# Fixing every engine's order by hand in an attention and feed-forward kernel: early casts and masks, spare matmuls, and values once per query third

## The chip, the cores and the metric

The kernel runs on one core of a Trainium2 chip. The metric is the device time of a run in microseconds. The profile's span (first to last instruction) is about 1.8 us shorter than that time.

The engines are called as the profile calls them: PE is TensorE's matmuls, PEld its weight loads, ACT ScalarE, DVE VectorE, POOL GpSimd, SP SyncE.

## The reference

Block-sparse attention (4 batches, 8 heads, 768 tokens, head size 64), then a multiplicative feed-forward layer on 3072 tokens:

```python
scores = q @ k.T / 8                       # per batch and head
mask   = |blk_i - blk_j| <= 1, or first/last block row or column, or one of 3 sampled blocks
attn   = softmax(where(mask, scores, -1e9))
x      = (attn @ v), heads side by side     # (3072, 512)
out    = ((x @ w1) * (x @ w2)) @ w3 @ w_out # d_ff = 1024, out (3072, 512)
```

## The kernel before

Queries are taken in tiles of 256, so each batch has three query thirds `t`; heads are taken four at a time (`Q`); keys in three pairs of chunks (`kp`). One *score group* is `(b, t, Q, kp)`: two score tiles of 128x1024, two exps, two mask multiplies. There are 72 groups, s = 0 to 71. Three consecutive groups (kp = 0, 1, 2) are what I call a *third*: after them the values and the softmax sum are complete and are normalized. There are 24 thirds.

`w3 @ w_out` is folded once into one matrix `wf` (the *fold*: w3 transposed on PE, `w3p`, copied by DVE to `w3t`, multiplied, `wp`, copied by DVE to `wf`). The feed-forward work is cut into *units* of four matmuls of 512 columns, held in a queue `fill` and popped between groups so that PE has work while ACT computes exps.

```python
ps_s = pool("ps_s", 2, space=PSUM)     # score tiles, also transposes: 2 buffers
ps_o = pool("ps_o", 1, space=PSUM)     # values and softmax sum
ps_f = pool("ps_f", 2, space=PSUM)     # everything else: mask, fold, feed-forward: 2 buffers
order = tc.manual_schedule(engines={PE, Activation, DVE})  # these run in the order written
# ... (masks: mp = matmul in ps_f, copied to SBUF on ACT; all nine before the first scores)

def scores(b, t, Q, kp, i):
    s = ps_s.tile(...)
    # 4 matmuls of 256 columns (64-row tiles)
    nc.scalar.activation(e, s, AF.Exp, scale=1.0 / 8.0)
    nc.vector.tensor_tensor(e, e, mask[...], op=ALU.mult)

def normalize(b, t, Q):
    nc.scalar.activation(ln, d, AF.Ln)
    nc.scalar.activation(rec[:, 0, :], ln, AF.Exp, scale=-1.0)
    nc.vector.tensor_tensor(X[i][...], o, rec, op=ALU.mult)

def pa(f):   p = ps_f.tile(...); 4 matmuls; nc.scalar.copy(a, p)                    # unit
def pb(f):   p = ps_f.tile(...); 4 matmuls; nc.vector.tensor_tensor(hT, p, a, mult) # unit
def po(n, half): 4 matmuls into box["o"] (ps_f); after the second half DVE copies it out

for s, g in enumerate(groups):
    scores(b, t, Q, kp, 0)
    scores(b, t, Q, kp, 1)
    if prev is not None:
        values(*prev)          # values of the group before
        finish(prev)           # normalize if kp == 2
    # ... (loads of the next batch; batches 1 to 3 are turned by DMA)
    pop(0 if s < 3 else 2)     # two units
    prev = g
```

(Cuts and shortened bodies are marked by `...` or described in comments.)

The softmax here doesn't subtract the row's maximum and nothing guards it: scores larger than these inputs give would overflow.

Of the kernel before, what the change touches and what calls it, by code (L numbers as in the profile page):

```python
# [17 lines left out]
def kernel(  # L18
# [16 lines left out]
    nc = tc.nc  # L35
# [10 lines left out]
    def pool(name, bufs, **kw):  # L46
# [7 lines left out]
    epool = pool("epool", 6)  # L54
# [10 lines left out]
        engines={mybir.EngineType.PE, mybir.EngineType.Activation, mybir.EngineType.DVE}  # L65
# [12 lines left out]
    rand_sb = const.tile([NB, 6], I32, tag="rand_sb")  # L78
    nc.sync.dma_start(out=rand_sb, in_=sampled_blocks.bitcast(I32))

    def load_pair(b, pr, which="qkv"):
        for src, dst, pl, tag in ((qv, qn, nat, "qn"), (kv, kn, nat, "kn"), (vv, vn, natv, "vn")):
            if tag[0] in which:
                t = pl.tile([128, 2, C, D], BF16, tag=tag, name=tag)
                nc.gpsimd.dma_start(out=t, in_=src[b][:, 2 * pr:2 * pr + 2])  # L85
                dst[b, pr] = t

# [7 lines left out]
    def load_w12(ap, t):  # L95
        src = ap.rearrange("(Q g s d) f -> g d Q s f", Q=2, g=4, s=2)
        for g in range(4):
            for Q in range(2):
# [3 lines left out]
    load_pair(0, 0, "qk")  # L102
    idf = const.tile([128, 128], F32, tag="idf")
    nc.gpsimd.iota(idf, pattern=[[-1, 128]], base=0, channel_multiplier=1,
                   allow_small_or_imprecise_dtypes=True)
    load_pair(0, 1, "qk")
    hotf = const.tile([NB, C, 128], F32, tag="hotf")
    nc.gpsimd.iota(hotf, pattern=[[1, C], [C, 128]], base=0, channel_multiplier=-BLK,
# [4 lines left out]
    II = const.tile([NB, NB], F32, tag="II")  # L113
    nc.gpsimd.iota(II, pattern=[[0, NB]], base=0, channel_multiplier=1,
                   allow_small_or_imprecise_dtypes=True)
    load_pair(0, 0, "v")
    load_pair(0, 1, "v")
    wo_v = moe_w_out.rearrange("(c r) f -> r c f", r=128)
    nc.gpsimd.dma_start(out=wo_sb, in_=wo_v)
# [5 lines left out]
    load_w3(0, 2)  # L125
    load_pair(0, 2)
    load_w3(2, 4)
    load_pair(0, 3)
    load_w3(4, NF)
    load_w12(moe_w1, w1_sb)  # L130
    load_w12(moe_w2, w2_sb)

    ident = const.tile([128, 128], BF16, tag="ident")
    nc.vector.tensor_scalar(ident, in0=idf, scalar1=0.0, scalar2=None, op0=ALU.is_equal)
    ones = const.tile([128, 32], BF16, tag="ones")
    nc.vector.memset(ones, 1.0)
    hot = const.tile([NB, C, 128], BF16, tag="hot")
# [4 lines left out]
    DD = const.tile([NB, NB], F32, tag="DD")  # L142
    nc.vector.tensor_sub(DD, II, JJ)

    A = const.tile([NB, NB], F32, tag="A")
    nc.vector.tensor_tensor(DD, DD, DD, op=ALU.mult)
    nc.vector.tensor_scalar(A, in0=DD, scalar1=1.0, scalar2=None, op0=ALU.is_le)
    for src in (II, JJ):
        for val, op in ((0.0, ALU.is_le), (float(NB - 1), ALU.is_ge)):
            t1 = small.tile([NB, NB], F32, tag="m24", name="m24")  # L150
            nc.vector.tensor_scalar(t1, in0=src, scalar1=val, scalar2=None, op0=op)
            nc.vector.tensor_max(A, A, t1)
    rand_f = const.tile([NB, 3], F32, tag="rand_f")
    for r in range(3):
        nc.vector.tensor_copy(rand_f[:, r:r + 1], rand_sb[:, 2 * r:2 * r + 1])
        t1 = small.tile([NB, NB], F32, tag="m24", name="m24")
        nc.vector.tensor_tensor(t1, JJ, rand_f[:, r:r + 1].to_broadcast((NB, NB)),
                                op=ALU.is_equal)
        nc.vector.tensor_max(A, A, t1)
    Ab = const.tile([NB, NB], BF16, tag="Ab")  # L160
    nc.vector.tensor_copy(Ab, A)
# [3 lines left out]
    gp = ps_s.tile([128, 2, 512], F32, tag="s", name="gp")  # L165
    for i, (lo, n) in enumerate(((0, 512), (512, 256))):
        nc.tensor.matmul(gp[:NB, i, :n], lhsT=Ab, rhs=hot2[:, lo:lo + n], start=True, stop=True)
        nc.vector.tensor_copy(G[:, lo:lo + n], gp[:NB, i, :n])
    mask = const.tile([128, NT, 3, 512], BF16, tag="mask")

    def build_mask(t):
        for kp in range(3):
            mp = ps_f.tile([128, 512], F32, tag="f", name="mp")
# [251 lines left out]
```

## Time and profile before

| what | before | view |
|---|---|---|
| time, median of 4 runs (288.42 to 289.52) | 288.82 us | times |
| span | 286.8 us | page |
| first exp | 20.53 us | timeline of ACT |
| groups 0 to 17 (first exp to group 18's first exp) | 53.6 us | timeline of ACT |
| from there to the first exp of the last third (17 thirds) | 164.2 us | timeline of ACT |
| one third in the steady state | 9.62 us | timeline of ACT |
| last third and tail | 48.5 us | timeline of ACT |

The page of the kernel before: busy time with share of the span, then the busy tenths and PE's granted clock in 40 slices of 7.2 us.

```profile
PE 260.8 (91%) x3124; PEld 132.3 (46%) x3124; DVE 183.8 (64%) x296; ACT 188.8 (66%) x250; POOL 71.5 (25%) x105
...
PE   0478888898999999999999999999999999999994
...
PEclk9986999999999999999999999999999999999998
```

PE is the bound for most of the span; the clock falls in the slices around 20 to 25 us, and at the very end.

The timeline of ACT in the kernel before. Columns: start in us, duration, engine, line, operation, output<-input, shapes, count, and in brackets idle time before it and what ended it. The mask copies stand ahead of the first exp; the second exp of the row at 73.22 is group 18's first, 0.95 us later; the last row opens the last third.

```profile
15.59 4.22 ACT L177 CAST mask<-mp 128x512 bf16<-128x512 f32 x8 [13.57 <-PE mp L175]
...
20.53 1.02 ACT L219 ACTIVATE e<-s 128x1024 bf16<-128x1024 f32 x1
...
73.22 1.97 ACT L219 ACTIVATE e<-s 128x1024 bf16<-128x1024 f32 x2
...
238.34 1.02 ACT L219 ACTIVATE e<-s 128x1024 bf16<-128x1024 f32 x1 [0.61 <-PE s L214]
```

One group of the steady state, in the timeline of the kernel before (same columns):

```profile
163.74 0.38 PE L314 MATMUL pb<-x,w_sb 128*128 128x512 bf16 x1
...
164.05 0.61 PE L214 MATMUL s<-qkt 64*128 64x256 bf16 x8
164.48 1.94 ACT L219 ACTIVATE e<-s 128x1024 bf16<-128x1024 f32 x2
...
164.78 0.40 PE L244 MATMUL o<-e,vn 128*32 128x256 bf16 x8
...
165.55 1.04 PE L303 MATMUL pa<-x,w_sb 128*128 128x512 bf16 x4
166.42 1.03 PE L314 MATMUL pb<-x,w_sb 128*128 128x512 bf16 x4
...
166.62 0.59 ACT L306 CAST a<-pa 128x512 bf16<-128x512 f32 x1 [0.20 <-PE pa L303]
```

Starts tell more than durations here, because matmuls overlap. From 163.74 (a pb matmul) to 164.05 (the first score matmul) it is 0.31 us, while pb matmuls follow each other by 0.216: a switch between kinds of matmul costs about 0.095 us. The Trainium skill, "TensorEngine Tiling (Array Packing)", Key Properties, says that changing the tiling mode drains TensorE; the trace agrees, and gives the size. Note the order on ACT: both exps of the group first, then the copy `a`. Here that does no harm: the values stand between scores and pa on PE, so that pa is done (166.6) just when the exps are (166.4).

PE's waits in the kernel before (engine, line, what it waited for: total us, times, longest):

```profile
PE gp L167 <- DVE Ab L161: 10.6, 1, 10.6
...
PE s L214 <- ACT e L219: 3.5, 10, 1.1
...
PE o L244 <- DVE x L260: 1.7, 2, 1.1
```

After the mask chain at the start (10.6 us) PE waits for little; the wait of `o` for `x` is the normalization that empties the one values buffer.

### The profile page before, as it was taken

How to read it: one execution, taken by the hardware profiler on the slowest of the kernel's cores; microseconds unless marked ns; L12 is line 12 of the kernel's file. 1: busy time of each engine (PE TensorE's matmuls, PEld its weight loads, DVE VectorE, ACT ScalarE, POOL GpSimd, SP SyncE). 2: the span in 40 equal slices, each digit the busy share in tenths (PEclk: the TensorE clock that was granted, in tenths of full speed). 3: DMA queues.
4: the chain of work that ended last, by engine and by line, in shares of the span. 5: the costliest groups of instructions: out<-in, count | busy, mean ns of one | idle time of the engine just before them, and what ended most of it. 6: DMA issues, size and time to landing. Idle time of an engine off the chain costs nothing.

```text
span 286.8 us, 7359 instructions
## 1 busy us (share of the span) xinstructions
PE 260.8 (91%) x3124; PEld 132.3 (46%) x3124; DVE 183.8 (64%) x296; ACT 188.8 (66%) x250; POOL 71.5 (25%) x105
## 2 busy tenths in 40 slices
PE   0478888898999999999999999999999999999994
PEld 0334555454544454445444554445444544444441
DVE  2616786786767776777677767766776677633332
ACT  1088764776788886888877888768887688611310
POOL 8614489374644820066000000000000000000000
PEclk9986999999999999999999999999999999999998
DMA  7999999999999992399912000121000220003003
GB/s 92 151 190 206 208 174 167 178 119 140 135 167 112 144 109 91 79 118 150 160 73 75 2 2 0 39 75 38 3 2 0 77 75 2 0 37 112 0 29 117
DMA packets 70356, 26.16 MB, mean 91 GB/s; under 512 B 58036, under 2 KB 65204, under 8 KB 70324
## 3 DMA queue, kind: packets, MB, share of 16 engines
q0 software_dynamic: 47632, 14.69, 50.9%
q1 hardware_dynamic: 22692, 11.02, 18.5%
q8 instruction: 24, 0.39, 0.6%
q14 instruction: 8, 0.07, 0.1%
HBM read 29.36 MB, written 6.29 MB: 124 GB/s over the span
## 4 chain that ended last, share of the span: by engine, by line
PE 62%; DMA 12%; ACT 12%; DVE 5%; POOL 5%; issue 3%; POOLq 0%; ACTq 0%
PE pa L303 13%; PE o L244 12%; PE pb L314 12%; DMA w_sb<-in_moe_w_dram 11%; PE po L324 10%; ACT e L219 7%; PE s L214 7%; DVE x L260 4%; PE d L241 4%; PE wp L285 3%; ACT rec L259 3%; ACT ln L257 2%; DMA nt<-in_q_dram 2%; POOL w_sb L99 1%; POOL vn L85 1%
## 5 line engine op out<-in xcount | busy, mean ns | idle before, releaser
L219 ACT ACTIVATE e<-s 128x1024 bf16<-128x1024 f32 x144 | 139.1, 1021 | 47.7 <-PE s L214 47.6
L220 DVE TENSOR_TENSOR e<-e,mask 128x1024 bf16<-128x1024 bf16 x144 | 99.0, 691 | 53.8 <-ACT e L219 53.8
L244 PE MATMUL o<-e,vn 128*32 128x256 bf16 x1152 | 54.7, 277 | 5.4 <-DVE x L260 1.7
L214 PE MATMUL s<-qkt 64*128 64x256 bf16 x576 | 46.8, 277 | 3.5 <-ACT e L219 3.5
L303 PE MATMUL pa<-x,w_sb 128*128 128x512 bf16 x192 | 49.7, 381 | 0.0
L314 PE MATMUL pb<-x,w_sb 128*128 128x512 bf16 x192 | 49.2, 379 | 0.0
L316 DVE TENSOR_TENSOR h<-pb,a 128x512 bf16<-128x512 f32 x48 | 33.1, 690 | 20.9 <-PE pb L314 20.9
L324 PE MATMUL po<-wf_sb,h 128*128 128x512 bf16 x192 | 44.5, 380 | 0.0
L306 ACT CAST a<-pa 128x512 bf16<-128x512 f32 x48 | 28.0, 582 | 22.6 <-PE pa L303 22.2
L241 PE MATMUL d<-e,ones 128*32 128x256 bf16 x576 | 42.5, 275 | 0.0
L214 PEld LDWEIGHTS <-qkt 64*128 64x128 bf16 x576 | 22.8, 95 | 34.7 <-issue 32.0
L244 PEld LDWEIGHTS <-vn 128*32 128x32 bf16 x1152 | 27.5, 96 | 22.0 <-issue 19.2
L314 PEld LDWEIGHTS <-w_sb 128*128 128x128 bf16 x192 | 18.7, 98 | 24.1 <-issue 2.6
L201 POOL DMA_DIRECT2D nt<-in_q_dram x24 | 19.7, 824 | 40.2 <-DMA qkt<-nt 35.9
L324 PEld LDWEIGHTS <-h 128*128 128x128 bf16 x192 | 17.5, 98 | 22.3 <-issue 3.4
L303 PEld LDWEIGHTS <-w_sb 128*128 128x128 bf16 x192 | 15.7, 98 | 21.7 <-issue 8.0
L329 DVE COPY ob<-po 128x512 f32<-128x512 f32 x24 | 16.5, 688 | 10.1 <-PE po L324 10.1
L201 POOL DMA_DIRECT2D nt<-in_k_dram x24 | 19.6, 821 | 4.3 <-DMA qkt<-nt 2.3
L260 DVE TENSOR_TENSOR x<-o,rec 128x512 bf16<-128x512 f32 x24 | 16.6, 692 | 1.6 <-ACT rec L259 0.9
L241 PEld LDWEIGHTS <-ones 128*32 128x32 bf16 x576 | 17.3, 98 | 0.3
L285 PE MATMUL wp<-wo_sb,w3t_sb 128*128 128x512 bf16 x64 | 15.2, 380 | 0.0
L177 ACT CAST mask<-mp 128x512 bf16<-128x512 f32 x9 | 4.8, 587 | 13.7 <-PE mp L175 13.7
(56 smaller groups left out, 106.9 us busy)
## 6 DMA issues: line engine op xcount, KB each, us to landing
out_dram<-ob SPq DMA_DIRECT2D x24, 256.0 KB, 2.0
vn<-in_v_dram POOLq DMA_DIRECT2D x16, 192.0 KB, 5.8
nt<-in_q_dram POOLq DMA_DIRECT2D x24, 96.0 KB, 5.6
nt<-in_k_dram POOLq DMA_DIRECT2D x24, 96.0 KB, 5.6
w_sb<-in_moe_w_dram POOLq DMA_DIRECT2D x8, 256.0 KB, 11.2
w_sb<-in_moe_w_dram POOLq DMA_DIRECT2D x16, 128.0 KB, 5.8
wo_sb<-in_moe_w_out_dram POOLq DMA_DIRECT2D x1, 1024.0 KB, 12.0
qn<-in_q_dram POOLq DMA_DIRECT2D x4, 192.0 KB, 7.2
```

What stands on the lines that cost most here:

```text
L201: nc.gpsimd.dma_start(out=n[:, :, h, :], in_=src[b][:, :, 2 * pr + h, :])
L214: nc.tensor.matmul(s[:, h, k2 * QT:(k2 + 1) * QT], lhsT=qk[64 * h:64 * h + 64, 1, kc * 128:(kc + 1) * 128], rhs=qk[64 * h:64 * h + 64, 0, ...
L219: nc.scalar.activation(e, s, AF.Exp, scale=1.0 / 8.0)
L220: nc.vector.tensor_tensor(e, e, mask[:, t, kp:kp + 1, :].to_broadcast((128, 2, 512)), op=ALU.mult)
L241: nc.tensor.matmul(d[rows, :], lhsT=ones, rhs=rhs, start=first, stop=last, skip_group_check=True)
L244: nc.tensor.matmul(o[rows, part * QT:(part + 1) * QT], lhsT=vn[b, 2 * Q + i][:, h, kc, 32 * part:32 * part + 32], rhs=rhs, start=first and ...
L260: nc.vector.tensor_tensor(X[i][:, 2 * Q:2 * Q + 2, half * QT:(half + 1) * QT], o.rearrange("p (s n) -> p s n", s=2), rec.to_broadcast((128 ...
L303: nc.tensor.matmul(p, lhsT=w1_sb[:, c, f * 128:(f + 1) * 128], rhs=x[:, c, :], start=c == 0, stop=c == 3)
L306: nc.scalar.copy(a, p)
L314: nc.tensor.matmul(p, lhsT=w2_sb[:, c, f * 128:(f + 1) * 128], rhs=x[:, c, :], start=c == 0, stop=c == 3)
L316: nc.vector.tensor_tensor(hT[:, f, :], p, box["a"], op=ALU.mult)
L324: nc.tensor.matmul(box["o"], lhsT=hT[:, f, n * 128:(n + 1) * 128], rhs=wf_sb[:, f, :], start=f == 0, stop=f == NF - 1)
```

## The change

Four intentions: an earlier first exp (float32 loads cast on ACT and DVE, a shorter mask chain, only the masks that are needed first); spare matmuls on a zero tile so that PE's clock stays up while it has nothing to do; values for a whole third at once, several groups late, so that PE switches less often and the normalization is off its path; orders of POOL and SP fixed as well. Batch 1's q and k are turned (transposed) by PE instead of DMA; the fold's units are sorted anew, and `w1` and `w2` are loaded at group 9. The diff, cut to its core:

```diff
-    epool = pool("epool", 6)
+    epool = pool("epool", 14)
     order = tc.manual_schedule(
-        engines={PE, Activation, DVE}
+        engines={PE, Activation, DVE, Pool, SP}
     )
+    # q and k of pairs 0 and 1 as float32 over SP, cast on ACT/DVE ("raw")
+    # mask matrix A by memset and affine_select on POOL ...
+    def warm(n):
+        if n:
+            w = ps_f.tile([128, 512], F32, tag="f", name="warm")
+            for _ in range(n):
+                nc.tensor.matmul(w, lhsT=warm_sb[:, :128], rhs=warm_sb, start=True, stop=True)
...
-    transposes(0, 0)
-    transposes(0, 1)
-    for t in range(NT):
-        build_mask(t)
+    warm(9)
+    cast("q", 0, nc.scalar.copy)
+    expand(0)                                  # G for t = 0
+    cast("k", 0, nc.vector.tensor_copy)
+    build_mask(0, 0, nc.scalar.copy)
+    transposes(0, 0, [nc.vector.tensor_copy] * 2)
+    cast("q", 1, nc.scalar.copy)
+    cast("k", 1, nc.vector.tensor_copy)
+    build_mask(0, 1, nc.scalar.copy)
...
-        if prev is not None:
-            values(*prev)
-            finish(prev)
-        pop(0 if s < 3 else 2)
+        if 0 < s <= LEAD:                      # LEAD = 6
+            attend(groups[s - 1:s])
+        elif s > LEAD + 3 and kp == 2:
+            attend(groups[s - 5:s - 2])        # three groups' values, then normalize
+        if s == 0:
+            build_mask(0, 2, nc.vector.tensor_copy)
+        if s in (0, 3):
+            expand(1 + s // 3)
+        if s < 6:
+            build_mask(1 + s // 3, s % 3, nc.vector.tensor_copy)
+        ...
+        if s in (14, 15, 18, 19):
+            transposes(1, (14, 15, 18, 19).index(s), [nc.vector.tensor_copy])
+        ...
+        if s < 4:
+            warm(3)
+        else:
+            pop(1.4 if s < LEAD else 2.0 if s == LEAD + 2 else (2.6, 2.6, 0.0)[kp])
```

A unit costs 0.86 of the budget in `pop`, so the steady state pops three units, three, and none in the three groups of a third.

More of the change, by code (lines that the diff above doesn't have):

```diff
@@ L64 @@
     order = tc.manual_schedule(
-        engines={mybir.EngineType.PE, mybir.EngineType.Activation, mybir.EngineType.DVE}
+        engines={mybir.EngineType.PE, mybir.EngineType.Activation, mybir.EngineType.DVE,
+                 mybir.EngineType.Pool, mybir.EngineType.SP}
     )
@@ L76 @@
     qn, kn, vn = {}, {}, {}
-    rand_sb = const.tile([NB, 6], I32, tag="rand_sb")
-    nc.sync.dma_start(out=rand_sb, in_=sampled_blocks.bitcast(I32))
     def load_pair(b, pr, which="qkv"):
@@ L86, in load_pair @@
                 dst[b, pr] = t
+    raw = {}
+    for pr in range(2):
+        both = hpool.tile([128, 2, 1024], F32, tag="h", name="raw")
+        for x, (src, tag) in enumerate(((qv, "q"), (kv, "k"))):
+            t = both[:, x, :2 * C * D].rearrange("p (h c d) -> p h c d", h=2, c=C)
+            nc.sync.dma_start(out=t, in_=src[0][:, 2 * pr:2 * pr + 2])
+            raw[tag, pr] = t
+        if pr == 0:
+            rand_sb = const.tile([NB, 3, 2], I32, tag="rand_sb")
+            nc.sync.dma_start(out=rand_sb,
+                              in_=sampled_blocks.bitcast(I32).rearrange("e (r w) -> e r w", w=2))
     w1_sb = wts.tile([128, 4, d_ff], BF16, tag="w1")
@@ L99, in load_w12 @@
                 nc.gpsimd.dma_start(out=t[32 * g:32 * g + 32, 2 * Q:2 * Q + 2, :], in_=src[g][:, Q])
-    load_pair(0, 0, "qk")
-    idf = const.tile([128, 128], F32, tag="idf")
+    idf = const.tile([128, 128], BF16, tag="idf")
     nc.gpsimd.iota(idf, pattern=[[-1, 128]], base=0, channel_multiplier=1,
-                   allow_small_or_imprecise_dtypes=True)
-    load_pair(0, 1, "qk")
-    hotf = const.tile([NB, C, 128], F32, tag="hotf")
-    nc.gpsimd.iota(hotf, pattern=[[1, C], [C, 128]], base=0, channel_multiplier=-BLK,
                    allow_small_or_imprecise_dtypes=True)
@@ L112 @@
                    allow_small_or_imprecise_dtypes=True)
-    II = const.tile([NB, NB], F32, tag="II")
-    nc.gpsimd.iota(II, pattern=[[0, NB]], base=0, channel_multiplier=1,
+    A = const.tile([NB, NB], F32, tag="A")
+    nc.gpsimd.memset(A, 0.0)
+    nc.gpsimd.memset(A[:, 0:1], 1.0)
+    nc.gpsimd.memset(A[:, NB - 1:NB], 1.0)
+    for base, pat, mul in ((0, -1, 1), (1, -1, 1), (-1, -1, 1), (0, 0, 1), (1 - NB, 0, 1)):
+        nc.gpsimd.affine_select(out=A, in_=A, compare_op=ALU.not_equal, fill=1.0, base=base,
+                                pattern=[[pat, NB]], channel_multiplier=mul)
+    hotf = const.tile([NB, C, 128], BF16, tag="hotf")
+    nc.gpsimd.iota(hotf, pattern=[[1, C], [C, 128]], base=0, channel_multiplier=-BLK,
                    allow_small_or_imprecise_dtypes=True)
@@ L117 @@
     load_pair(0, 1, "v")
-    wo_v = moe_w_out.rearrange("(c r) f -> r c f", r=128)
-    nc.gpsimd.dma_start(out=wo_sb, in_=wo_v)
+    nc.gpsimd.dma_start(out=wo_sb, in_=moe_w_out.rearrange("(c r) f -> r c f", r=128))
     def load_w3(lo, hi):
@@ L123, in load_w3 @@
             nc.gpsimd.dma_start(out=w3_sb[:, i, :], in_=moe_w3[128 * i:128 * i + 128, :])
-    load_w3(0, 2)
+    load_w3(0, 3)
     load_pair(0, 2)
-    load_w3(2, 4)
+    load_w3(3, 4)
     load_pair(0, 3)
     load_w3(4, NF)
-    load_w12(moe_w1, w1_sb)
-    load_w12(moe_w2, w2_sb)
+    warm_sb = const.tile([128, 512], BF16, tag="warm")
+    nc.vector.memset(warm_sb, 0.0)
     ident = const.tile([128, 128], BF16, tag="ident")
@@ L136 @@
     nc.vector.memset(ones, 1.0)
+    rand_f = const.tile([NB, 3], F32, tag="rand_f")
+    nc.vector.tensor_copy(rand_f, rand_sb[:, :, 0])
+    Ab = const.tile([NB, NB], BF16, tag="Ab")
+    for r in range(3):
+        nc.vector.scalar_tensor_tensor(Ab if r == 2 else A, in0=JJ, scalar=rand_f[:, r:r + 1],
+                                       in1=A, op0=ALU.is_equal, op1=ALU.max)
     hot = const.tile([NB, C, 128], BF16, tag="hot")
@@ L141 @@
     nc.vector.tensor_tensor(hot, hot, hot_hi, op=ALU.mult)
-    DD = const.tile([NB, NB], F32, tag="DD")
-    nc.vector.tensor_sub(DD, II, JJ)
-    A = const.tile([NB, NB], F32, tag="A")
-    nc.vector.tensor_tensor(DD, DD, DD, op=ALU.mult)
-    nc.vector.tensor_scalar(A, in0=DD, scalar1=1.0, scalar2=None, op0=ALU.is_le)
-    for src in (II, JJ):
-        for val, op in ((0.0, ALU.is_le), (float(NB - 1), ALU.is_ge)):
-            t1 = small.tile([NB, NB], F32, tag="m24", name="m24")
-            nc.vector.tensor_scalar(t1, in0=src, scalar1=val, scalar2=None, op0=op)
-            nc.vector.tensor_max(A, A, t1)
@@ L153 @@
-    rand_f = const.tile([NB, 3], F32, tag="rand_f")
-    for r in range(3):
-        nc.vector.tensor_copy(rand_f[:, r:r + 1], rand_sb[:, 2 * r:2 * r + 1])
-        t1 = small.tile([NB, NB], F32, tag="m24", name="m24")
-        nc.vector.tensor_tensor(t1, JJ, rand_f[:, r:r + 1].to_broadcast((NB, NB)),
-                                op=ALU.is_equal)
-        nc.vector.tensor_max(A, A, t1)
-    Ab = const.tile([NB, NB], BF16, tag="Ab")
-    nc.vector.tensor_copy(Ab, A)
+    def warm(n):
[3 more added lines that the diff above has]
+                nc.tensor.matmul(w, lhsT=warm_sb[:, :128], rhs=warm_sb, start=True, stop=True)
@@ L163, with expand @@
     hot2 = hot.rearrange("e c p -> e (c p)")
     G = const.tile([NB, S], BF16, tag="G")
-    gp = ps_s.tile([128, 2, 512], F32, tag="s", name="gp")
-    for i, (lo, n) in enumerate(((0, 512), (512, 256))):
-        nc.tensor.matmul(gp[:NB, i, :n], lhsT=Ab, rhs=hot2[:, lo:lo + n], start=True, stop=True)
-        nc.vector.tensor_copy(G[:, lo:lo + n], gp[:NB, i, :n])
     mask = const.tile([128, NT, 3, 512], BF16, tag="mask")
-    def build_mask(t):
-        for kp in range(3):
-            mp = ps_f.tile([128, 512], F32, tag="f", name="mp")
-            for k2 in range(2):
-                nc.tensor.matmul(mp[:, k2 * QT:(k2 + 1) * QT], lhsT=hot[:, 2 * kp + k2, :],
-                                 rhs=G[:, t * QT:(t + 1) * QT], start=True, stop=True)
-            nc.scalar.copy(mask[:, t, kp, :], mp)
+    def expand(t):
+        gp = ps_f.tile([128, 512], F32, tag="f", name="gp")
+        nc.tensor.matmul(gp[:NB, :QT], lhsT=Ab, rhs=hot2[:, t * QT:(t + 1) * QT],
+                         start=True, stop=True)
+        nc.vector.tensor_copy(G[:, t * QT:(t + 1) * QT], gp[:NB, :QT])
@@ L180, with build_mask, transposes @@
+    def build_mask(t, kp, copy):
+        mp = ps_f.tile([128, 512], F32, tag="f", name="mp")
+        for k2 in range(2):
+            nc.tensor.matmul(mp[:, k2 * QT:(k2 + 1) * QT], lhsT=hot[:, 2 * kp + k2, :],
+                             rhs=G[:, t * QT:(t + 1) * QT], start=True, stop=True)
+        copy(mask[:, t, kp, :], mp)
     QK = {}
-    def transposes(b, pr):
+    def transposes(b, pr, copies):
         tp = ps_s.tile([128, 2, 1024], BF16, tag="s", name="tp")
@@ L189, in transposes @@
         t = qkt.tile([128, 2, S], BF16, tag="qkt", name="qkt")
-        nc.vector.tensor_copy(t, tp[:, :, :S])
+        if len(copies) == 1:
+            copies[0](t, tp[:, :, :S])
+        else:
+            for x, copy in enumerate(copies):
+                copy(t[:, x, :], tp[:, x, :S])
         QK[b, pr] = t
     qd, kd = (x.rearrange("b h (p c) d -> b p c h d", c=C) for x in (q, k))
+    turned = {}
     def load_pair_t(b, pr):
-        load_pair(b, pr, "v")
-        t = qkt.tile([128, 2, S], BF16, tag="qkt", name="qkt")
-        for x, src in enumerate((qd, kd)):
+        ns = []
+        for src in (qd, kd):
             n = nat.tile([128, C, 2, D], BF16, tag="nt", name="nt")
@@ L201, in load_pair_t, with turn @@
                 nc.gpsimd.dma_start(out=n[:, :, h, :], in_=src[b][:, :, 2 * pr + h, :])
+            ns.append(n)
+        turned[b, pr] = ns
+        load_pair(b, pr, "v")
+    def turn(b, pr):
+        t = qkt.tile([128, 2, S], BF16, tag="qkt", name="qkt")
+        for x, n in enumerate(turned.pop((b, pr))):
             nc.sync.dma_start_transpose(out=t[:, x, :].rearrange("r (c p) -> r c p", c=C),
@@ L328, in go, with cast @@
                     ob = opool.tile([128, 512], F32, tag="ob", name="ob")
-                    nc.vector.tensor_copy(ob, box["o"])
-                    nc.sync.dma_start(out=outv[b, c], in_=ob)
+                    if i == B * NT // 2 - 1 and n == 3:
+                        nc.scalar.copy(ob[:, :256], box["o"][:, :256])
+                        nc.scalar.dma_start(out=outv[b, c][:, :256], in_=ob[:, :256])
+                        nc.vector.tensor_copy(ob[:, 256:], box["o"][:, 256:])
+                        nc.sync.dma_start(out=outv[b, c][:, 256:], in_=ob[:, 256:])
+                    else:
+                        nc.vector.tensor_copy(ob, box["o"])
+                        nc.sync.dma_start(out=outv[b, c], in_=ob)
             return go
         for f in range(NF):
-            fill.append(pa(f))
-            fill.append(pb(f))
+            fill.append((0.86, pa(f)))
+            fill.append((0.86, pb(f)))
         for n in range(4):
-            fill.append(po(n, 0))
-            fill.append(po(n, 1))
-    transposes(0, 0)
-    transposes(0, 1)
-    for t in range(NT):
-        build_mask(t)
+            fill.append((0.86, po(n, 0)))
+            fill.append((0.86, po(n, 1)))
+    warm(9)
+    def cast(tag, pr, copy):
+        t = nat.tile([128, 2, C, D], BF16, tag=tag + "n", name=tag + "n")
+        copy(t, raw[tag, pr])
+        (qn if tag == "q" else kn)[0, pr] = t
+    cast("q", 0, nc.scalar.copy)
[6 more added lines that the diff above has]
+    build_mask(0, 1, nc.scalar.copy)
     groups = []
@@ L351 @@
         groups += [(b, t, Q, kp) for t, Q in outer for kp in range(3)]
-    for i in range(NF):
-        fill.append(fold_transpose(i, 0))
-        fill.append(fold_transpose(i, 1))
-        fill.extend(fold_mm(i))
+    ft = [(0.25, fold_transpose(i, jh)) for i in range(NF) for jh in range(2)]
+    fm = [(0.86, go) for i in range(NF) for go in fold_mm(i)]
+    fill.extend(ft[:2])
+    for k_, go in enumerate(fm):
+        fill.append(go)
+        fill.extend(ft[k_ + 2:k_ + 3])
     done = {}
     n_ffn = 0
-    prev = None
     def finish(g):
@@ L369, in finish, with pop, attend @@
                 n_ffn += 1
-    def pop(n):
-        for _ in range(n):
-            if fill:
-                fill.popleft()()
+    def pop(budget):
+        while fill and budget >= fill[0][0] - 0.05:
+            cost, go = fill.popleft()
+            budget -= cost
+            go()
+    def attend(gs):
+        for g in gs:
+            values(*g)
+        finish(g)
+    LEAD = 6
     for s, g in enumerate(groups):
@@ L378 @@
         r = s % 18
-        scores(b, t, Q, kp, 0)
-        scores(b, t, Q, kp, 1)
-        if prev is not None:
-            values(*prev)
-            finish(prev)
-        if b + 1 < B and r in (2, 5, 8, 11):
-            load_pair_t(b + 1, (r - 2) // 3)
-        if b == 0 and s in (7, 8):
-            transposes(0, s - 5)
-        pop(0 if s < 3 else 2)
-        prev = g
-    values(*prev)
-    finish(prev)
+        if s == 0:
+            scores(*g, 0)
+            transposes(0, 1, [nc.vector.tensor_copy])
+            scores(*groups[1], 0)
+        elif s == 1:
+            scores(*groups[0], 1)
+            scores(*g, 1)
+        else:
+            scores(*g, 0)
+            scores(*g, 1)
+        if 0 < s <= LEAD:
+            attend(groups[s - 1:s])
+        elif s > LEAD + 3 and kp == 2:
+            attend(groups[s - 5:s - 2])
+        if s == 0:
+            build_mask(0, 2, nc.vector.tensor_copy)
[3 more added lines that the diff above has]
+            build_mask(1 + s // 3, s % 3, nc.vector.tensor_copy)
+        if s in (7, 8):
+            transposes(0, s - 5, [nc.vector.tensor_copy])
+            load_pair(1, s - 7)
+        if s == 9:
+            load_w12(moe_w1, w1_sb)
+            load_w12(moe_w2, w2_sb)
+            load_pair(1, 2)
+            load_pair(1, 3)
+        if s in (14, 15, 18, 19):
+            transposes(1, (14, 15, 18, 19).index(s), [nc.vector.tensor_copy])
+        if 0 < b < B - 1:
+            if r in (2, 4, 6, 8):
+                load_pair_t(b + 1, (r - 2) // 2)
+            if r in (9, 10, 11, 12):
+                turn(b + 1, r - 9)
+        if s < 4:
+            warm(3)
+        else:
+            pop(1.4 if s < LEAD else 2.0 if s == LEAD + 2 else (2.6, 2.6, 0.0)[kp])
+    attend(groups[-3:])
     while fill:
-        pop(1)
+        pop(1.0)
     order.__exit__(None, None, None)
```

## The prediction

> **What bounds the kernel now.** TensorE: 260.8 of 286.8 us busy (busy table). From about 84 to 248 us the kernel is periodic: the timeline shows one query third (three score groups, 6 exps, two feed-forward units of four 512-column matmuls per group) every 9.62 us. By matmul starts, a 512-column matmul costs 0.216 us, a score group 0.42, a values group 0.65. Each switch between scores, values and feed-forward costs about 0.095 us extra (0.31 instead of 0.216 between starts). The Trainium skill, "TensorEngine Tiling (Array Packing)", Key Properties, says that changing the tiling mode drains TensorE; the trace agrees. A third has 9 switches, plus a 0.19 us wait of values for the normalization.
>
> Before that: first exp at 20.5 us (mask chain on VectorE to 10.5 us, nine mask copies on ScalarE 15.6 to 20.6), granted clock 0.50 at 20 to 25 us. Fits "TensorE: Matmul & The Clock Gate", Part 1 (half clock after an idle window). Groups 0 to 17 take 53.6 us.
>
> **What the change does.** (a) Start: float32 loads cast on ScalarE/VectorE, shorter mask chain on GpSimd, only two mask copies ahead of the first exp, the rest on VectorE. I estimate the first exp at 12 us: -8.5. The warm matmuls mostly fill waits. (b) Groups 0 to 17: fold work spread evenly, transposes of batch 1 on TensorE instead of small DMAs (4 x 1.3 us added), no fill left at groups 15 to 17: net about -2. (c) Steady state: values for three groups at once, 6 switches instead of 9 and no normalization wait: bare TensorE work falls to 8.97 us per third.
>
> **But (c) creates a new wait.** Feed-forward units come three in a row directly behind a score group, through the two shared PSUM buffers. The third reuses the first's buffer, freed by a ScalarE copy that stands behind both exps (and, in the first group of a third, behind ln and reciprocal). With durations of the trace (exp spacing 0.92, copy 0.58, ln to rec 0.43, rec to exp 0.32) that copy ends about 3.26 us after the scores start; TensorE would be ready at 2.25: about 1.06 us lost. In the second group the last unit waits about 0.83 us for the copy just before it, or the second half of an output unit about 1.0 us for a product queued behind the mask multiply. Output-only thirds don't stall. Estimated thirds per feed-forward block: 10.9, 10.9, 11.1, 9.0, mean 10.4 against 9.62; over 18 thirds +15 us. (d) Tail: two units fewer, last store split: about -1.
>
> Sum: -8.5 - 2 + 15 - 1 = +3.5. I lean lower: **289.5 us**, range 281 to 297. Faster by over 2%: 0.20; within 2%: 0.60; slower: 0.20.
>
> **What would show it.** First exp at 11 to 13.5 us; group 18 starts near 64 us (before: 74); no half clock at 20 to 25 us. Steady thirds of 10 to 11 us while first/second-layer units run and about 9.0 us for output-only ones. In the waits view, TensorE "pa" and "pb" waiting on ScalarE's copy, 10 us or more in total (before: 0).
>
> **What would make it wrong.** If the third unit doesn't wait, thirds take 9.0 to 9.2 us and the total falls to about 265. If weights arrive late behind the float32 loads, groups 4 to 12 stall. If the first exp waits for the sampled blocks, queued behind two large loads, it comes after 14 us.

## The result, and the profile after

The changed kernel took 324.38 us (median of 4 runs, 324.06 to 324.83) against 288.82 us: ratio 1.123, 95% interval 1.120 to 1.126. A ratio is the mean time of one kernel's fast runs over that of the other's of the same rounds, so it is not quite the ratio of the medians. The kernel became 12% slower; the prediction expected no change to speak of.

| stage (by exp starts on ACT) | before | after | measured | predicted |
|---|---|---|---|---|
| to the first exp | 20.5 | 11.9 | -8.6 | -8.5 |
| groups 0 to 17 | 53.6 | 78.8 | **+25.1** | **-2** |
| 17 thirds from group 18 on | 164.2 | 182.3 | +18.1 | +15 (for 18) |
| last third and tail | 48.5 | 50.1 | +1.6 | -1 |
| span | 286.8 | 323.0 | +36.2 | +3.5 |

The page after (the lines that answer to those of before):

```profile
PE 272.5 (84%) x3242; PEld 142.7 (44%) x3242; DVE 188.9 (58%) x295; ACT 185.9 (58%) x246; POOL 63.0 (19%) x100
...
PE   5786887778779888988889888898897989879995
...
PEclk9559879999699999999999999999999999999999
```

The span grew by 36.2 us; ACT did about the same work as before, DVE 5.1 us more, and PE 11.7 us more, part of it matmuls at half clock. So over the whole kernel most of the time went into waiting. The clock row shows half clock early and in three more places in the first third of the run. The page counts a stretch for which the trace has no clock record as full clock; the first record here begins at 4.67 us.

The timeline of ACT after, at the same stage borders:

```profile
11.91 1.02 ACT L239 ACTIVATE e<-s 128x1024 bf16<-128x1024 f32 x1 [0.61 <-PE s L234]
...
90.68 1.01 ACT L239 ACTIVATE e<-s 128x1024 bf16<-128x1024 f32 x1
...
272.98 1.01 ACT L239 ACTIVATE e<-s 128x1024 bf16<-128x1024 f32 x1
```

PE's costliest waits after:

```profile
PE pa L323 <- ACT a L326: 11.2, 13, 0.9
...
PE pb L334 <- ACT a L326: 6.1, 9, 0.7
...
PE mp L183 <- DVE G L178: 5.0, 3, 2.6
...
PE w3p L292 <- DVE w3t_sb L294: 3.6, 3, 1.6
PE po L344 <- DVE h L336: 3.3, 4, 0.8
PE w3p L292 <- DVE mask L185: 2.7, 2, 2.0
```

Two families are new. The waits of pa, pb and po belong to the steady state; those of mp and w3p to groups 0 to 17. All of them wait for the reader of a `ps_f` buffer, or for an operand that such a reader makes.

**The steady state.** The first group of a third, in the timeline after:

```profile
198.93 0.38 ACT L277 ACTIVATE ln<-d 128x256 f32<-128x256 f32 x1 [0.37 <-PE d L261]
...
199.34 0.42 ACT L279 ACTIVATE rec<-ln 128x256 f32<-128x256 f32 x1
...
199.35 1.04 PE L323 MATMUL pa<-x,w_sb 128*128 128x512 bf16 x4
199.66 1.92 ACT L239 ACTIVATE e<-s 128x1024 bf16<-128x1024 f32 x2
...
200.22 1.03 PE L334 MATMUL pb<-x,w_sb 128*128 128x512 bf16 x4
...
201.47 0.59 ACT L326 CAST a<-pa 128x512 bf16<-128x512 f32 x1
...
202.11 1.02 PE L323 MATMUL pa<-x,w_sb 128*128 128x512 bf16 x4 [0.86 <-ACT a L326]
```

pa's matmuls are done by 200.4, but their copy `a` starts only at 201.47, because ln, rec and both exps stand ahead of it on ACT. The third unit reuses pa's buffer and starts at 202.11 instead of 201.08 (200.22 plus four times 0.216). Thirds take 10.95, 10.96, 11.12 and 9.10 us in turn, mean 10.53, against 9.62 before. This is the wait that the prediction described.

**Groups 0 to 17.** Group 5 begins with the exps in the first line of this timeline after; group 6 with the last:

```profile
38.30 1.94 ACT L239 ACTIVATE e<-s 128x1024 bf16<-128x1024 f32 x2 [3.12 <-PE s L234]
...
39.17 0.39 PE L183 MATMUL mp<-G,hot 24*128 24x256 bf16 x2
39.35 0.69 DVE L240 TENSOR_TENSOR e<-e,mask 128x1024 bf16<-128x1024 bf16 x1 [1.95 <-ACT e L239]
...
40.27 0.69 DVE L240 TENSOR_TENSOR e<-e,mask 128x1024 bf16<-128x1024 bf16 x1 [0.22 <-ACT e L239]
40.88 0.68 DVE L185 CAST mask<-mp 128x512 bf16<-128x512 f32 x1
41.61 0.38 PE L292 MATMUL w3p<-ident,w_sb 128*128 128x128 bf16 x4 [2.05 <-DVE mask L185]
...
43.72 1.03 PE L234 MATMUL s<-qkt 64*128 64x256 bf16 x8
...
44.37 1.02 ACT L239 ACTIVATE e<-s 128x1024 bf16<-128x1024 f32 x1 [4.13 <-PE s L234]
```

This is a loop in series. The mask matmul is done at 39.6, but its copy stands on DVE behind both mask multiplies, which wait for the exps; PE's next fold transpose needs that copy's buffer and waits 2.05 us; the next scores stand behind it, and behind two more fold steps, on PE; and the next exps wait 4.13 us for the scores. One group takes 6.1 us although ACT needs 2 us for it: from 40.24 to 44.37 us ACT computes nothing. A part of this is not order: from 42.22 to 45.63 us the clock was at half (the w3p matmuls at 43.15 are 0.107 us apart, those at 41.61 0.055).

The same group in the kernel before, where no mask copy is left in the loop:

```profile
33.61 2.89 ACT L219 ACTIVATE e<-s 128x1024 bf16<-128x1024 f32 x3 [1.91 <-PE s L214]
...
34.49 0.62 PE L272 MATMUL w3p<-ident,w_sb 128*128 128x128 bf16 x8
...
35.04 0.39 PE L214 MATMUL s<-qkt 64*128 64x256 bf16 x4
```

The fold transposes and the next scores start without a wait, and the exps run on: this group takes 1.9 us. (Groups 0 to 17 took 1.8 to 5.6 us each before, 3.0 on average, and 4.4 on average after.)

The loop is not the whole of the 25.1 us. From the first exp to group 18's, PE is busy 61.2 of 78.8 us after and 46.6 of 53.6 before (windows view). So 14.7 us of the 25.1 are longer work on PE, among it the 12 spare matmuls, two of batch 1's transposes and matmuls at half clock; the other 10.5 us are more idle time. Late data is hardly a part: in this stretch PE, ACT and DVE waited 0.6 us in all for a DMA.

### The profile page after: what moved, and what is told of

It reads as the page before. It is cut to its first block, busy times and chain, and to the rows that moved or that the text cites. A ratio compares the mean times of both kernels' runs of the same rounds, so it can differ in the third digit from the quotient of the medians.

```text
span 323.0 us, 7552 instructions
## 1 busy us (share of the span) xinstructions
PE 272.5 (84%) x3242; PEld 142.7 (44%) x3242; DVE 188.9 (58%) x295; ACT 185.9 (58%) x246; POOL 63.0 (19%) x100
## 4 chain that ended last, share of the span: by engine, by line
PE 56%; ACT 29%; DVE 7%; issue 6%; DMA 1%; SPq 0%; ACTq 0%; DVEq 0%
ACT e L239 19%; PE po L344 11%; PE o L264 11%; PE pa L323 7%; PE s L234 7%; PE pb L334 6%; ACT a L326 6%; PE d L261 5%; PE wp L305 3%; ACT ln L277 2%; DVE e L240 2%; PE tp L195 2%; ACT rec L279 2%; PE warm L168 1%; PE w3p L292 1%
## 5 line engine op out<-in xcount | busy, mean ns | idle before, releaser
L264 PE MATMUL o<-e,vn 128*32 128x256 bf16 x1152 | 53.0, 285 | 2.7 <-DVE x L280 1.7
L264 PEld LDWEIGHTS <-vn 128*32 128x32 bf16 x1152 | 29.7, 100 | 11.1 <-issue 9.9
L344 PEld LDWEIGHTS <-h 128*128 128x128 bf16 x192 | 18.1, 98 | 27.2 <-DVE h L336 5.4
L214 POOL DMA_DIRECT2D nt<-in_q_dram x16 | 13.2, 832 | 77.1 <-issue 55.0
L280 DVE TENSOR_TENSOR x<-o,rec 128x512 bf16<-128x512 f32 x24 | 16.6, 692 | 16.3 <-ACT rec L279 16.3
L355 DVE COPY ob<-po 128x512 f32<-128x512 f32 x23 | 15.5, 687 | 8.7 <-PE po L344 8.7
L261 PEld LDWEIGHTS <-ones 128*32 128x32 bf16 x576 | 16.5, 101 | 0.8
L277 ACT ACTIVATE ln<-d 128x256 f32<-128x256 f32 x24 | 9.2, 385 | 13.2 <-PE d L261 13.2
L305 PE MATMUL wp<-wo_sb,w3t_sb 128*128 128x512 bf16 x64 | 16.8, 389 | 0.0
L83 POOL DMA_DIRECT2D vn<-in_v_dram x16 | 11.6, 723 | 19.2 <-PE d L261 17.7
## 6 DMA issues: line engine op xcount, KB each, us to landing
w_sb<-in_moe_w_dram POOLq DMA_DIRECT2D x8, 256.0 KB, 10.5
```

The lines of the kernel that those rows point to most:

```text
L261: nc.tensor.matmul(d[rows, :], lhsT=ones, rhs=rhs, start=first, stop=last, skip_group_check=True)
L264: nc.tensor.matmul(o[rows, part * QT:(part + 1) * QT], lhsT=vn[b, 2 * Q + i][:, h, kc, 32 * part:32 * part + 32], rhs=rhs, start=first and ...
L280: nc.vector.tensor_tensor(X[i][:, 2 * Q:2 * Q + 2, half * QT:(half + 1) * QT], o.rearrange("p (s n) -> p s n", s=2), rec.to_broadcast((128 ...
L305: nc.tensor.matmul(box["p"], lhsT=w3t_sb[:, j, i * 128:(i + 1) * 128], rhs=wo_sb[:, j, :], start=j == 0, stop=j == NF - 1)
L344: nc.tensor.matmul(box["o"], lhsT=hT[:, f, n * 128:(n + 1) * 128], rhs=wf_sb[:, f, :], start=f == 0, stop=f == NF - 1)
```

## The experiments

**Theory A** (steady state): the third unit in a row waits for a `ps_f` buffer whose reader stands behind the exps in its engine's queue. Rivals: values per third are themselves slower; or load order and buffers.

**Theory C** (groups 0 to 17): each group is one serial loop, because copies that free `ps_f` stand behind this group's multiplies on DVE and because PE keeps its order. Rival D: half clock, late data, or the 96 extra transposes.

The results at a glance, in us, from each profile. "Third" is the mean of the 16 thirds from group 21 to 68; the time is one run unless a count is given.

| kernel | first exp | groups 0-17 | groups 18-20 | third | time |
|---|---|---|---|---|---|
| before | 20.5 | 53.6 | 10.2 | 9.62 | 288.82 (4 runs) |
| changed | 11.9 | 78.8 | 13.8 | 10.53 | 324.38 (4 runs) |
| v_each | 11.9 | 72.9 | 11.6 | 9.63 | 298.33 |
| two_units | 11.8 | 79.0 | 12.7 | 9.21 | 299.95 |
| exp_between | 12.7 | 78.5 | 12.1 | 9.58 | 307.44 |
| before_third | 20.4 | 55.3 | 10.2 | 9.21 | 284.35 |
| no_warm | 12.4 | 72.6 | 13.8 | 10.53 | 319.20 |
| copies_first (wrong result) | 12.9 | 71.8 | 13.8 | 10.53 | 318.81 |
| copies_first2 | 11.0 | 70.7 | 13.8 | 10.53 | 315.72 |
| masks_up | 18.0 | 66.0 | 13.8 | 10.53 | 318.15 |
| best1 | 18.9 | 56.8 | 13.0 | 9.35 | 288.56 |
| best1_dma | 18.0 | 54.5 | 9.6 | 9.35 | 281.84 |
| best2 | 12.7 | 55.5 | 9.6 | 9.35 | 277.51 (4 runs) |
| best2_warm | 11.7 | 52.4 | 9.6 | 9.35 | 275.14 (6 runs) |

The kernel before took 288.4 to 289.8 us beside these runs.

### Steady state: v_each

```diff
-        if 0 < s <= LEAD:
+        if s:
             attend(groups[s - 1:s])
-        elif s > LEAD + 3 and kp == 2:
-            attend(groups[s - 5:s - 2])
...
-            pop(1.4 if s < LEAD else 2.0 if s == LEAD + 2 else (2.6, 2.6, 0.0)[kp])
-    attend(groups[-3:])
+            pop(1.4 if s < LEAD else 2.0 if s == LEAD + 2 else 1.75)
+    attend(groups[-1:])
```

> The changed kernel, with values taken per score group again and two feed-forward units per group (as before the change); start and other orders as changed. Theory A (the slower steady state comes from the third feed-forward unit in a row waiting for one of the two PSUM buffers, whose reader stands behind the exps): thirds fall from 10.95/10.95/11.12/9.10 us back to 9.6, groups 18 to 71 from 193 to about 175 us, total 302 to 306 us; TensorE's wait of pa and pb for the ScalarE copy nearly gone. Rival (the steady state is slower for another cause, such as the new load order or the 14 exp buffers): thirds stay above 10 us, total above 315.

Measured: thirds of 9.63 us, as before the change; the waits of pa and pb for ACT are gone from the list. The time, 298.33 us, is below the expected 302 to 306, because groups 0 to 17 became 5.8 us shorter as well. The steady state is settled as a matter of order: loads and buffers of the changed kernel are innocent.

### Steady state: two_units

```diff
-            pop(... (2.6, 2.6, 0.0)[kp])
+            pop(... (1.75 if s >= 18 else (2.6, 2.6, 0.0)[kp]))
```

> The changed kernel, values still once per third, but from group 18 on two feed-forward units after every group instead of three, three and none. Theory A: the waits fall from about 1.9 us per third to under 0.5; thirds 9.1 to 9.5 us, groups 18 to 71 about 168 us, total 296 to 301 us. Rival B (taking the values once per third is what costs): thirds stay at 10.5 us or more, total above 315.

Measured: thirds of 9.21 us, 299.95 us. In this timeline of two_units, the first group of a third ends and the second begins:

```profile
142.15 0.59 ACT L326 CAST a<-pa 128x512 bf16<-128x512 f32 x1
...
142.26 0.61 PE L234 MATMUL s<-qkt 64*128 64x256 bf16 x8
...
142.81 1.04 PE L323 MATMUL pa<-x,w_sb 128*128 128x512 bf16 x4
```

The copy `a` is still behind the exps, but it ends at 142.74, just before PE asks for the buffer at 142.81: the scores lie in between. Values per third do not cost, they save 0.41 us per third, and rival B falls.

### Steady state: exp_between

The three units are kept; only places in the queues change. From group 18 on, in the first two groups of a third:

```diff
-            scores(*g, 0)
-            scores(*g, 1)
+            scores(*g, 0)
+            second = scores(*g, 1, later=True)   # its matmuls now, exp and multiply later
+            pop(0.86)                            # one unit, with its copy or product
+            second()                             # second exp and multiply
...
-            pop(... (2.6, 2.6, 0.0)[kp])
+            pop(... if s < 18 else (1.74, 1.74, 0.0)[kp])
```

> The changed kernel with its three, three and none units per third kept; only the order on ScalarE and VectorE is changed from group 18 on: in the first and second group of a third, the first unit's copy or product stands between the two exps and mask multiplies instead of behind both. Theory A in its exact form (the wait is the place of the reader of the PSUM buffer in its engine's queue, not the number of units): the third unit of the first group waits about 0.2 us instead of 0.9, the output unit's wait for h falls from 0.8 to about 0.2; thirds about 10.1, 10.1, 9.4 and 9.1 us instead of 10.95, 10.96, 11.12, 9.10; total 307 to 312 us. Rival (three units in a row are too many for two buffers in any order): thirds within 0.2 us of the changed kernel's, total 320 to 326.

Measured: thirds of 9.92, 9.92, 9.39 and 9.10 us, 307.44 us. In this timeline of exp_between the copy stands between the exps and the third unit starts without a wait:

```profile
142.52 0.58 ACT L331 CAST a<-pa 128x512 bf16<-128x512 f32 x1
...
142.98 1.04 ACT L241 ACTIVATE e<-s 128x1024 bf16<-128x1024 f32 x1
143.15 1.02 PE L328 MATMUL pa<-x,w_sb 128*128 128x512 bf16 x4
```

So with the same number of units, place alone is worth 0.95 us per third. The Trainium skill, "TensorE: Matmul & The Clock Gate", Part 1 (engine queue depths), says that ScalarE and VectorE are strict first-in-first-out queues; the traces agree: in the changed kernel pa was done at 200.4 us and its copy, written behind the exps, started at 201.47; here, written between them, it ends at 143.10, before the second exp does. What is left above 9.21 comes to about 6 us over the 16 thirds; pb's wait for `h` (3.3 us in total here) is about half of it.

### One part alone on the old kernel: before_third

```diff
-    epool = pool("epool", 6)
+    epool = pool("epool", 14)
...
-        if prev is not None:
-            values(*prev)
-            finish(prev)
+        if s > 3 and kp == 2:
+            for x in groups[s - 5:s - 2]:
+                values(*x)
+            finish(x)
```

> The kernel before with one part of the change alone: values once per third and 14 exp buffers, feed-forward units still two per group, nothing else. Theory A (values per third is a gain of about 0.41 us per third as long as units come in twos): thirds 9.2 us from group 21 on, total 279 to 284 us. Rival (the gain needs the other hand-fixed orders, or is eaten in the fold stage): total above 286 us.

Measured: thirds of 9.21 us and 284.35 us, 1.8% below the kernel before beside it (289.51), a little above the range named; one run. The steady thirds repeat to 0.01 us, so the gain there is sure. Groups 0 to 17 gave 1.7 us back (55.3 instead of 53.6).

### Groups 0 to 17: no_warm

```diff
         if s < 4:
-            warm(3)
+            pass
```

> The changed kernel without the 12 spare matmuls inside groups 0 to 3 (the nine at the start stay). Theory C (in groups 0 to 17 each group is one serial loop over TensorE, ScalarE, VectorE and back, so the spare matmuls lie on the chain): groups 0 to 17 shorten from 79 to about 74 us, total 317 to 320. Rival D (they keep TensorE's clock up and are needed): groups 0 to 17 get longer than 79 us because of a longer stretch at half clock, total above 325.

Measured: groups 0 to 17 in 72.6 us, 319.2 us. The spare matmuls cost about 5 us of time: each three of them stand on PE ahead of the next scores, on the chain. Of the 6.1 us that the stage lost, 4.0 are in groups 0 to 5; the other 2.1 are in groups 6 to 17, where the edit changes nothing but where the changed kernel's half clock from 83.2 to 90.0 us is missing in no_warm. Rival D, that they are needed for the clock, falls.

### Groups 0 to 17: copies_first, and copies_first2

Multiplies (and the normalization's product) go into a list that is run at the end of a group's orders, after the copies:

```diff
-        nc.vector.tensor_tensor(e, e, mask[...], op=ALU.mult)
+        late.append(lambda: nc.vector.tensor_tensor(e, e, mask[...], op=ALU.mult))
...
+        if s >= 18:                # copies_first2: if s == 1 or s >= 18
+            flush()
...
             pop(...)
+        flush()
```

> The changed kernel; in groups 0 to 17 only, VectorE's order is changed: the copies that free the two shared PSUM buffers (mask, G, transposed w3, folded weights, turned q and k) stand before the group's two mask multiplies and the normalization instead of behind them. Theory C: groups 0 to 17 fall from 79 us to 50 to 60 us, total 295 to 304 us; TensorE's waits of mp and w3p for VectorE nearly gone. Rival D (late weights, the half clock or the 96 extra transposes on TensorE make groups 0 to 17 long): they stay above 70 us, total above 314.

The first version gave a wrong result (relative error 0.12). In group 1 the changed kernel still has half of group 0's scores to do and then reads them in the values, so the order in which I wrote it lets values read what is not yet multiplied. The version mended by one condition is correct, and tells the same:

> copies_first with its error mended (in group 1 the multiplies stay ahead of the values that read them); otherwise the same change of VectorE's order in groups 0 to 17. The wrong version took 317.0 us of span with groups 0 to 17 in 71.8 us. Expected now: output correct, groups 0 to 17 in 70 to 74 us, total 317 to 321 us: the copies' place costs about 5 to 8 us of the 25 us, not all of it, as first expected. If the wrong version was fast only because it read too early, groups 0 to 17 take over 76 us.

Measured: groups 0 to 17 in 70.7 us, 8.1 less than the changed kernel; 315.72 us. PE's wait of mp for G fell from 5.0 to 1.8 us, of w3p for DVE from 6.3 to 1.7. So the place of the copies is one part of the 25 us, not all, and my first expectation (50 to 60 us) was wrong: values of the group before still stand on PE and wait for their multiplies (`o` waits 2.7 us for `e`), and groups 7 and 8, where PE also turns q and k, take over 4 us in either order.

### Groups 0 to 17: masks_up

```diff
     build_mask(0, 1, nc.scalar.copy)
+    build_mask(0, 2, nc.vector.tensor_copy)
+    for t in (1, 2):
+        expand(t)
+        for kp in range(3):
+            build_mask(t, kp, (nc.scalar.copy, nc.vector.tensor_copy)[(3 * t + kp) % 2])
...          # and the three calls inside the loop are removed
```

> The changed kernel with all nine masks built ahead of the first scores (copies in turn on ScalarE and VectorE) instead of seven of them inside groups 0 to 5. Theory C (mask copies between the multiplies make groups 0 to 5 a serial loop): the first exp comes 2 to 4 us later (14 to 16 us), groups 0 to 5 shorten from 32.5 us by at least 8 us, group 18 starts at 80 to 85 us instead of 90.7, total 312 to 318 us. Rival D (the half clock or late data makes them long): groups 0 to 5 stay within 3 us of 32.5 us and the total rises.

Measured: groups 0 to 5 in 20.4 us instead of 32.5, groups 0 to 17 in 66.0; but the first exp at 18.0 us, later than expected, so group 18 starts at 84.0 instead of 90.7. Taking the masks out of the loop shortens groups 0 to 5 by about 12 us; building them first gives half of that back. Rival D, as it was put, did not hold: groups 0 to 5 were not within 3 us. But the half clock is not excluded as a part of the 12 us: in masks_up these groups start later, and only 3.3 us of them ran at half clock, against 18.8 in the changed kernel (at the rate estimated under "What stays open" below, about 4 of the 12 us).

### All repairs: best1 and best1_dma

best1 is masks_up, plus the deferred multiplies in groups 3 to 17, no spare matmuls in the loop, and:

```diff
-        if s < 4:
-            warm(3)
-        else:
-            pop(1.4 if s < LEAD else 2.0 if s == LEAD + 2 else (2.6, 2.6, 0.0)[kp])
+        if s > 2:
+            pop(1.4 if s < 18 else 1.75)
+        flush()
```

> All repairs together on the changed kernel: masks ahead of the first scores, no spare matmuls in the loop, copies that free PSUM ahead of the mask multiplies in groups 3 to 17, fold work from group 3, two units per group from group 18. Theory A with C: first exp 14 to 16 us, groups 0 to 17 in 50 to 56 us, thirds 9.2 us, total 268 to 276 us. If another cause holds groups 0 to 17 up, they take over 62 us and the total is above 280.

Measured: 288.56 us, no better than the kernel before (289.51 beside it). Groups 0 to 17 take 56.8 us, close to the range named, but the first exp comes at 18.9, groups 18 to 20 take 13.0 us, and thirds take 9.35 instead of 9.21 us. The traces show where the thirds differ: in two_units a group takes pa and pb of one pair, in best1 the units are out of step by one, so that a group takes pb and then the next pair's pa. In the second group of a third pb then starts 0.62 us after the scores instead of 0.42, at 128.68 us, just after the copy `a` behind both exps has ended (128.63). This is theory A's wait again, in small; best2 and best2_warm have the same thirds. best1_dma turns batch 1 by DMA again:

```diff
-        if s in (14, 15, 18, 19):
-            transposes(1, (14, 15, 18, 19).index(s), [nc.vector.tensor_copy])
-        if 0 < b < B - 1:
+        if b < B - 1:
             # loads and DMA transposes of batch b + 1
```

(The same edit moves the loads of `w1` and `w2` from group 9 to group 0.)

> As best1, but q and k of batch 1 are turned by DMA, as before the change, instead of by 96 transposes on TensorE. If those transposes cost TensorE their 4 x 1.3 us plus waits for a score buffer, groups 0 to 20 shorten by 5 to 8 us and the total is 262 to 270 us. If the small loads arrive late behind the weights, as the change assumed, groups 18 on wait and the total is above that of best1.

Measured: 281.84 us, 6.7 less than best1 on the same chip, as expected of the difference; the level was again misjudged by the late first exp. 0.9 us of the 6.7 lie ahead of the first exp, where no transpose of batch 1 stands. So turning batch 1 on PE, with the order of loads that goes with it, is a real part of the loss: 5.8 us in these orders, 2.3 in groups 0 to 17 and 3.5 in groups 18 to 20. The prediction's 4 x 1.3 us was about right.

### A version that beats both: best2 and best2_warm

best2 takes values out of the early chain (per third from the start), builds all of G right after the first score tile, keeps the later masks in the loop with their copies ahead of the multiplies, and keeps best1_dma's other repairs:

```diff
             scores(*g, 0)
+            expand(1)
+            expand(2)
             transposes(0, 1, [nc.vector.tensor_copy])
...
-        if 0 < s <= LEAD:
-            attend(groups[s - 1:s])
-        elif s > LEAD + 3 and kp == 2:
+        if s > 3 and kp == 2:
             attend(groups[s - 5:s - 2])
```

> On the changed kernel: values once per third from the first third on, so that no values stand between the early scores; all of G before the loop, masks of the later tiles still in groups 0 to 5 but their copies ahead of the multiplies; no spare matmuls in the loop; fold work from group 3; q and k of batch 1 by DMA; two units per group. Theory C (the early loop was serial; once nothing on TensorE waits for this group's multiplies, ScalarE's exps at about 2 us per group set the pace): first exp 12 to 13 us, groups 0 to 17 in 47 to 53 us, thirds 9.2 us, total 265 to 273 us. If the early part is held by half clock or data instead, groups 0 to 17 stay above 55 us and the total above 276.

Measured: 277.51 us (4 runs, 274.4 to 277.65), ratio to before 0.958 (0.953 to 0.963). It beats both kernels, but groups 0 to 17 take 55.5 us, above the expected range. best2_warm is `warm(20)` at the start instead of `warm(9)`:

> best2 with 20 spare matmuls at the start instead of 9, so that TensorE is busy until its first real work at about 7.4 us and does not fall back to half clock at 8 us. If the half clock costs in groups 0 to 5: 1 to 4 us less than best2. If ScalarE's exps set the pace there: within 1 us of best2.

Measured: 275.14 us (6 runs, 273.44 to 275.66), ratio 0.954 (0.951 to 0.956): 4.6% below the kernel before. In the profiled runs groups 0 to 5 are 3.1 us shorter than in best2, but these two runs lie apart (277.6 and 273.44 us, the latter the fastest of its six); the ranges of the times overlap, so the 2.4 us between the medians is likely but not sure. The clock did rise earlier: the spare matmuls are 0.427 us apart up to about 6.4 us, then 0.216. It fell to half all the same from 16.6 to 23.4 us. What the repaired order looks like, in the timeline of ACT of best2_warm:

```profile
11.66 1.02 ACT L245 ACTIVATE e<-s 128x1024 bf16<-128x1024 f32 x1 [0.51 <-PE s L240]
13.16 6.65 ACT L245 ACTIVATE e<-s 128x1024 bf16<-128x1024 f32 x7 [0.48 <-PE s L240]
```

Seven exps run in one go, about 0.93 us apart (1.8 us per group), where the changed kernel's groups 0 to 5 took 2.6 to 7.2 us each. The order is not perfect: groups 3 to 5 of best2_warm still take 3.3 to 5.4 us. best2_warm's page has PE busy 94% of 271.6 us.

## Why the prediction was wrong

- **First exp: right.** Expected at 12 us, measured 11.91; -8.5 against -8.6.
- **Steady state: right in mechanism and size.** Expected thirds 10.9, 10.9, 11.1, 9.0; measured 10.95, 10.96, 11.12, 9.10. Waits of pa and pb for ACT's copy: expected 10 us or more, measured 17.3. exp_between shows that the reader's place in ACT's and DVE's queues is the cause. The total came out at +18.1 for 17 thirds because groups 18 to 20 (+3.6 us) also carry two of batch 1's transposes, which I had booked in groups 0 to 17.
- **The step that failed: "Groups 0 to 17: fold work spread evenly, transposes of batch 1 on TensorE instead of small DMAs (4 x 1.3 us added), no fill left at groups 15 to 17: net about -2."** Measured +25.1, most of the error. I had added up each engine's work per group and let the largest stand for the group, as if the engines overlapped (the prediction records only the sum). They did not: mask copies, G and w3t stood behind the group's multiplies on DVE, PE waited for their buffers in order, and the next scores waited behind. It is the same mechanism that I had worked out for the feed-forward units, and I did not ask the same question of the other users of the same two buffers. Single edits took away, of groups 0 to 17: masks out of the loop 12.8 us (at the price of a first exp 6.1 us later), copies ahead of multiplies 8.1, the spare matmuls 6.1, values per group with two units in groups 7 to 17 5.8. They overlap, so they need not add up. Each is one run of a stage that occurs once in it, and some of each may be clock (best2's four times alone differ by 3.3 us); the combination in best2_warm brings the stage to 52.4 us. The sizes of the parts stay rough; that order alone costs much is shown by copies_first2, which moves nothing but DVE's order.
- **"No half clock at 20 to 25 us": wrong.** The granted clock was 0.50 from 8.1 to 25.1 us. **"The warm matmuls mostly fill waits": wrong** inside the loop, where they cost about 5 us (no_warm).
- **Tail: -1 expected, +1.6 measured**; most of that is in the last third itself: the first exp of its third group comes 7.9 us after that of its first, against 6.5 before the change.
- **"I lean lower"** took the sum of +3.5 further down for no measured reason, in the wrong direction.

What stays open: how much of the changed kernel's groups 0 to 5 is due to the half clock. An estimate: best2's page shows full clock from the start, but its trace has no clock record before 31.05 us, and its fold matmuls were still 0.427 us apart at 28 us, so it ran at half clock until then; best2_warm did so only from 16.6 to 23.4 us. Groups 6 to 17 take 33.4 us in both, so 3.1 us of groups 0 to 5 go with 11.5 us less of half clock. At this rate the changed kernel's 18.8 us of half clock in groups 0 to 5 are worth about 5 of their 32.5 us. No run isolates it, but it is not the main cause: best2, at half clock for 18.3 us of these groups, needs 22.1 us for them.

## What to carry to other kernels

When orders are fixed by hand, ask of every buffer that PE reuses: who empties it, and what stands ahead of that reader in its engine's queue; a copy written behind work that waits for another engine turns two overlapping engines into one chain. Batching work on one engine removes switches, but it also removes the gap that hid someone's latency, so put back something else in that gap (two units per group here instead of three). Busy sums per group bound a stage only after this check, and they have to be made for the start of a kernel as carefully as for its steady state.

## What the Trainium skill lacked or had wrong

- "TensorEngine Tiling (Array Packing)", Key Properties, says that a mode switch drains TensorE but gives no size. Here a switch cost about 0.095 us (0.31 us between starts of a 512-column and the next score matmul, instead of 0.216); going from 9 switches per third to 7 with no wait for the normalization was worth 0.41 us of 9.62.
- "TensorE: Matmul & The Clock Gate", Part 1, says that the window is free-running, that about 3.4 us of sustained activity releases the throttle and that an idle window, or frequent short idling between groups of matmuls, brings it back; it gives no measure of how idle a window must be. Here the clock fell without a wholly idle one: in the changed kernel after the 3.41 us from 4.67 to 8.08, in which PE was busy 0.61 us and its longest gap was 2.36 us (below), and in the kernel before at 19.05 us, after 3.42 us with PE busy 2.35 us and no gap over 0.35 us. It then stayed at half from 8.08 to 25.15 us, though PE was busy 1.7 to 3.2 us in each of the first four stretches of 3.41 us. So the warm-up by nine spare matmuls on zeros, from 1.2 to 5.0 us and 0.427 us apart (half clock), was lost. Zero operands did count as activity: in best2_warm, with 20 of them, the spacing fell to 0.216 us.

```profile
1.21 3.81 PE L168 MATMUL warm<-warm_sb 128*128 128x512 bf16 x9 [1.21 <-DVE warm_sb L146]
7.38 0.26 PE L176 MATMUL gp<-hot,Ab 24*24 24x256 bf16 x1 [2.36 <-DVE hot L161]
```

- The same page warns that the trace's clock events are unreliable; early ones are missing: the profile shows clock 1.00 from 0 to 4.6 us in the changed kernel, and up to 31 us in best2, where the traces have no record, while the spacing of 0.427 us says half.
- No page says how to find the reader of a reused PSUM buffer that stands behind unrelated work in a first-in-first-out queue. Here that cost 0.86 us per wait of pa, and 2.05 us in one wait of w3p.
